# Batch 0 of a pooled-attention and feed-forward kernel: three fp32 loads on SyncE's queue, v in two loads, pooled products in bank tiles of their own

## The chip, the core and the metric

The kernel runs on one core of a Trainium2 chip. The metric is the device time of one execution in microseconds (us). The engines are named as in the profile: PE (TensorE, matrix products), DVE (VectorE), ACT (ScalarE), POOL (GpSimd) and SP (SyncE, which only issues transfers). Each engine works through its own list of instructions in order, and semaphores join the lists. Matrix products are written to PSUM[...]; DVE and ACT read them from there.

## The reference

Two steps follow one another. The first is attention with pooled keys and values. Eight batches of eight heads have 576 tokens of 64 numbers; eight neighbouring rows of k and of v are averaged, so that each head has 72 pooled rows.

```python
k_p = k.reshape(B, H, Sp, pool, D).mean(axis=3)
v_p = v.reshape(B, H, Sp, pool, D).mean(axis=3)
scores = scale * np.matmul(q, k_p.transpose(0, 1, 3, 2))
scores = scores - np.max(scores, axis=-1, keepdims=True)
attn = np.exp(scores)
attn = attn / (np.sum(attn, axis=-1, keepdims=True) + 1e-09)
return np.matmul(attn, v_p)
```

The second treats the 4608 tokens of 512 numbers as rows of x:

```python
h = x @ w_in            # 512 x 2048
g = h * np.cos(h)
return g @ w_out        # 2048 x 512
```

All inputs are fp32. The kernel computes with bf16 operands and fp32 sums.

## The kernel before, in words

The 4608 tokens are nine chunks of 512. For each chunk `t` the kernel does the up stage (`up_mm`, line 291, sixteen groups of four products of 128x128 by 512, two groups to a pair of banks `banks[fp % 3]`), the cosine on ACT and the product on DVE (`up_g`, line 301), and the down stage (`down_mm`, line 309, 64 products). The attention of batch `t + 1` is woven into the down stage of chunk `t` through the list `fill`, whose first entry is the number of the down product ahead of which a piece stands. The order of the work is written out by hand; no planner changes it.

**Batch 0 has nothing to hide behind.** Its attention is the head of the kernel (lines 396 to 420), and the change is there. The steps are these. `pool_k_mm` (line 150) multiplies k rows by a matrix of zeros and ones, `groups`, and so gives the pooled, transposed keys; one call treats two pairs of heads. The two heads of a pair lie in the lower and the upper 64 rows of the array. `put_kk` (line 128) copies the result from PSUM to `kk`, four copies to a call, since each head is wanted in both halves of the partitions. `q_transpose_mm` (line 189) transposes q in 18 blocks of 128 columns; blocks 0 to 8 are the first two head pairs. `scores` (line 204) multiplies and calls the exponential on ACT (line 218). `sums_first` (line 260) makes the sums of the exponentials and their inverse by a logarithm and an exponential on ACT (lines 270 and 271). `pool_v_mm` (line 160) pools v for all four head pairs at once into `vz`. `values_then` (line 274) multiplies by the pooled v, and DVE scales the result into `xT` (line 282). The four units of `us` are head pairs 0 and 1 for token segments 0 and 1, then head pairs 2 and 3 for both segments. `up_mm(0, 0, 0, 2)` and `up_mm(0, 1, 0, 2)` need only the first two units; the up products with `ki` 2 and 3 need the last two.

**Loads.** All loads but one go through POOL's queue (`nc.gpsimd.dma_start`), which turns fp32 into bf16 on the way. The one exception is the first half of k for batch 0: line 342 loads it as fp32 over SP's queue into the space of `g_sb`, which is not used until chunk 0's cosine, and ACT turns it into bf16 (line 343). POOL issues, in order: half of q, the constants for `groups` (lines 348 and 351), the second halves of k and of q, v, the identity, three parts of `w_in`, k and q of batch 1, the last part of `w_in`, the rest of q, `w_out` part 0, v of batch 1, two clearings of `kp2`, and `w_out` parts 1 to 3. Eight semaphores take turns on this queue, so each load waits, before it is issued, for the eighth load ahead of it. The loads are carried out in order by sixteen DMA engines.

`groups` is made on DVE (lines 361 to 365), ahead of the clearing of `vz[0]` and two small constants. `warm_up` (line 388) runs products on a constant tile whose result nobody reads.

Of the kernel before, what the change touches and what calls it, by code (L numbers as in the profile page):

```python
# [9 lines left out]
FP32 = mybir.dt.float32  # L10
# [4 lines left out]
POOL = 8  # L15
# [4 lines left out]
def kernel(  # L20
# [59 lines left out]
    def even_view(src, b, j0=0, j1=KCH):  # L80
        return src[b, 2 * j0:2 * j1].rearrange("(j a) (p t) d -> (a p) j (t d)", a=2, t=ROW)
# [43 lines left out]
    def v_part(b):  # L125
        return vz[b % 2][:, :, 0:4:3, :]

    def put_kk(b, ps, pj0, pj1, copy):
        dst = kk[b % 2].rearrange("p (j a) n -> p j a n", a=2)
        for a in range(2):  # L130
            for r in range(2):
                copy(out=dst[half[r], pj0:pj1, a, 0:Sp], in_=ps[half[a]])

    def pool_add(b, which):

        st = staged.pop((which, b))
# [10 lines left out]
            s = s.rearrange("p (j a) t d -> p j a t d", a=2)  # L147
            add(out=v_part(b), in0=s[..., 0, :], in1=s[..., 1, :], op=ADD)

    def pool_k_mm(b, bank, pj0, pj1):  # L150

        kb = staged["k", b]
        ps = bank[:, 0:(pj1 - pj0) * Sp].rearrange("p (j n) -> p j n", n=Sp)
        for pj in range(pj0, pj1):
            for t in range(ROW):
                for rows in half:
                    nc.tensor.matmul(ps[rows, pj - pj0, :], lhsT=kb[rows, pj, t, :], rhs=groups[rows, t, :],
                                     start=(t == 0), stop=(t == ROW - 1))
        return lambda copy: put_kk(b, ps, pj0, pj1, copy)

    def pool_v_mm(b, pair):
        vb = staged["v", b]
        for t in range(ROW):
            for hp, rows in enumerate(half):
                nc.tensor.matmul(pair[:Sp, hp, 0:KCH * D], lhsT=groups[rows, t, :], rhs=vb[rows, :, t, :],
                                 start=(t == 0), stop=(t == ROW - 1))
        nc.vector.tensor_copy(out=v_part(b).rearrange("p j a d -> p a j d"),
                              in_=pair[:Sp, :, 0:KCH * D].rearrange("p a (j d) -> p a j d", j=KCH))

    def k_transpose(b):  # L170
        nc.sync.dma_start_transpose(out=kk[b % 2], in_=kp2[b % 2].rearrange("p h s d -> p (h s d)"))
# [160 lines left out]


    EX = 5
    warm = consts.tile([128, 512], BF16, name="warm")
    nc.vector.memset(warm, 1.0)
    exp_tables()

    kv_even_tiles(0)
    q_tile(0)  # L340
    k_first = g_sb.rearrange("p f n -> p (f n)").bitcast(FP32)[:, 0:2 * ROW * D]
    nc.sync.dma_start(out=k_first.rearrange("p (j n) -> p j n", j=2), in_=even_view(k, 0, 0, 2))
    nc.scalar.copy(out=staged["k", 0][:, 0:2].rearrange("p j t d -> p (j t d)"), in_=k_first)
    load_even(staged["q", 0], 0, q, 0, 2)

    row_of = consts.tile([128, ROW], FP32, name="row_of")
    for rows in half:
# [4 lines left out]
                   allow_small_or_imprecise_dtypes=True)  # L352
    load_even(staged["k", 0], 0, k, 2, 4)
    load_even(staged["q", 0], 0, q, 2, 4)
    load_even(staged["v", 0], 0, v)
    identity = consts.tile([128, 128], BF16, name="identity")
    make_identity(nc, identity)
    dist = consts.tile([128, ROW, Sp], FP32, name="dist")
    sign = consts.tile([128, ROW, Sp], FP32, name="sign")
    groups = consts.tile([128, ROW, Sp], BF16, name="groups")  # L360
    nc.vector.tensor_tensor(out=dist, in0=row_of.unsqueeze(2).to_broadcast([128, ROW, Sp]),
                            in1=first_of.unsqueeze(1).to_broadcast([128, ROW, Sp]), op=mybir.AluOpType.subtract)
    nc.vector.scalar_tensor_tensor(out=sign, in0=dist, scalar=1.0 - POOL, in1=dist, op0=ADD,
                                   op1=mybir.AluOpType.mult)
    nc.vector.tensor_scalar(out=groups, in0=sign, scalar1=0.0, scalar2=None, op0=mybir.AluOpType.is_le)
    nc.vector.memset(vz[0], float(POOL))
    ones = consts.tile([128, D], BF16, name="ones")
    nc.vector.memset(ones, float(POOL))
    gate = consts.tile([1, 1], BF16, name="gate")
    half_pi = consts.tile([128, 1], FP32, name="half_pi")  # L370
    nc.vector.memset(half_pi, math.pi / 2.0)

    kv_even_tiles(1)
    q_tile(1)
# [5 lines left out]
    load_even(staged["q", 1], 1, q, 2, 4)  # L380
    load_w_out(0)
    load_even(staged["v", 1], 1, v)
    for i in range(2):
        nc.gpsimd.memset(kp2[i], 0.0)
    for cg in range(1, 4):
# [2 lines left out]
    def warm_up(n, bank):  # L388

        for i in range(n):  # L390
            nc.tensor.matmul(bank, lhsT=warm[:, 0:128], rhs=warm)

    vec, act = nc.vector.tensor_copy, nc.scalar.copy
    us = BY_HEADS

    warm_up(10, obanks[0])
    pool_k_mm(0, obanks[1], 0, 2)(vec)
    warm_up(2, banks[1][:, 0, :])
    puts = q_transpose_mm(0, banks[2][:, 0, :], 0, 5), q_transpose_mm(0, obanks[0], 5, 9)
    puts[0](vec)  # L400
    puts[1](act)
    warm_up(2, banks[1][:, 0, :])
    scores(0, us[0], banks[0])
    scores(0, us[1], banks[1])
    pool_k_mm(0, obanks[1], 2, 4)(vec)
    sums_first(0, us[0], banks[0][:, 0, :])
    puts = q_transpose_mm(0, banks[2][:, 0, :], 9, 14), q_transpose_mm(0, obanks[0], 14, 18)
    puts[0](vec)
    puts[1](act)
    sums_first(0, us[1], obanks[1])  # L410
    scores(0, us[2], banks[0])
    scores(0, us[3], banks[2])
    nc.vector.memset(vz[1], float(POOL))
    pool_v_mm(0, banks[1])
    sums_first(0, us[2], obanks[0])
    values_then(0, us[0], obanks[1])
    values_then(0, us[1], banks[1][:, 0, :])
    sums_first(0, us[3], banks[2][:, 0, :])
    values_then(0, us[2], obanks[1])
    values_then(0, us[3], obanks[0])  # L420
    up_mm(0, 0, 0, 2)
    up_mm(0, 1, 0, 2)
    sin_tables()
# [1 line left out]
    for t in range(NT):  # L425
        b = t + 1
        if t > 0:

            up_mm(t, 0, 0, 2)
            up_mm(t, 1, 0, 2)  # L430
        for fp in range(FFCH // 2):
            up_mm(t, fp, 2 if fp < 2 else 0)
            between = ()
            if t == 0:
                if fp == 4:
                    puts = pool_k_mm(1, obanks[0], 0, 2), pool_k_mm(1, obanks[1], 2, 4)
# [12 lines left out]
        mms = [(ms, fc) for ms in range(4) for fc in range(FFCH)]  # L449
        if t == 0:  # L450
            mms = [(ms, fc) for hm in range(2) for cg in range(4) for ms in range(2 * hm, 2 * hm + 2)
                   for fc in range(4 * cg, 4 * cg + 4)]


        def S_(n, bank):
            return lambda: scores(b, us[n], banks[bank])

        later = []

        def V_(n, bank, wait=None):  # L460
            return lambda: values(b, us[n], banks[bank], wait)

        fill = []
        if t < B:
            exp_tables()
            fill = [(1, lambda: scores(t, REST, banks[2])), (12, lambda: values(t, REST, banks[1]))]
        if t == 0:
            fill[1:] = [(2, S_(0, 0)), (8, lambda: pool_v_mm(1, banks[1])), (8, lambda: values(t, REST, banks[2])),
                        (11, S_(1, 0)), (13, V_(0, 1)), (18, S_(2, 2)), (21, V_(1, 0, later)), (26, S_(3, 1)),
                        (32, lambda: later.pop()()), (32, V_(2, 2)), (40, V_(3, 0))]  # L470
# [64 lines left out]
```

The softmax here doesn't subtract the row's maximum and nothing guards it: scores larger than these inputs give would overflow.

## Time and profile before

| What | Value |
|---|---|
| Median of five runs | 303.48 us (303.41 to 308.05) |
| The profiled execution | 303.48 us, of which its span 301.7 us |
| Granted TensorE clock | 1.0 over the span |
| PE busy | 291.4 us, 97% of the span |
| ACT, DVE, POOL busy | 205.9, 171.6, 129.9 us |
| First up product of chunk 0 | 17.42 us into the span |
| First down product of chunk 0 | 33.66 us into the span |
| HBM read, written | 36.70 MB, 9.44 MB |

The span counts from the first instruction of the profiled execution to its last. A timeline line gives the start and the duration, then engine, line, operation and tiles, the number of instructions merged into it, and in brackets for how long the engine was idle before it and what ended that. In a table of windows each engine has its busy time and number of instructions; the last two columns are the mean share of the sixteen DMA engines that had a packet under way and the bytes written per second. A casting load counts with its bf16 bytes, half of what it reads.

### The profile page before, as it was taken

What the parts mean: (1) busy time and instruction counts of PE and PEld (TensorE: products, weight loads), DVE (VectorE), ACT (ScalarE), POOL (GpSimd) and SP (SyncE); (2) the same over time, 40 slices, a digit from 0 to 9 for tenths busy, and PEclk for the clock granted to TensorE, in tenths of its full rate; (3) what the DMA queues carried; (4) which work ended last, traced back from release to release, by engine and by line L of the source; (5) the groups of instructions that cost most, each with busy time, mean ns of one, the idle gap of its engine ahead of it and who ended that gap; (6) DMA issues with size and microseconds to landing.
All of it is one profiled execution on the core that took longest, in us unless ns stands there. A gap on an engine that the chain in (4) does not pass through costs nothing.

```text
span 301.7 us, 4567 instructions
## 1 busy us (share of the span) xinstructions
PE 291.4 (97%) x1766; PEld 142.4 (47%) x1798; DVE 171.6 (57%) x211; ACT 205.9 (68%) x255; POOL 129.9 (43%) x92
## 2 busy tenths in 40 slices
PE   7799999999999999999999999999999999999994
PEld 2545544444544554455444544455445544444443
DVE  6558546574467446754675566654675476415612
ACT  3886897469866987688768877789578966506500
POOL 8553017984973398339823990399200000000000
PEclk9999999999999999999999999999999999999999
DMA  7999999739436951796069707791811130131032
GB/s 143 200 207 206 209 203 200 159 47 183 99 70 119 177 111 44 135 169 129 16 157 150 137 20 171 105 166 35 149 24 35 37 70 0 34 73 35 0 72 70
DMA packets 44005, 32.91 MB, mean 109 GB/s; under 512 B 22096, under 2 KB 39248, under 8 KB 43984
## 3 DMA queue, kind: packets, MB, share of 16 engines
q0 software_dynamic: 19744, 18.07, 38.2%
q1 hardware_dynamic: 24080, 14.42, 20.4%
q8 instruction: 14, 0.23, 0.3%
q10 hardware_dynamic: 160, 0.13, 0.2%
q14 instruction: 7, 0.06, 0.1%
HBM read 36.70 MB, written 9.44 MB: 153 GB/s over the span
## 4 chain that ended last, share of the span: by engine, by line
PE 83%; DMA 11%; POOL 2%; ACT 2%; issue 1%; DVE 0%; POOLq 0%; ACTq 0%
PE obank L310 38%; PE bank L297 37%; DMA w_out_sb<-in_moe_w_out_dram 6%; DMA w_in_sb<-in_moe_w_in_dram 5%; PE bank L241 5%; PE bank L211 3%; PE bank L328 1%; ACT ex L218 1%; POOL q_b L84 1%; POOL kv_st L84 1%; POOL w_in_sb L112 0%; ACT L285 0%; ACT cos L304 0%; POOL identity masks.py:197 0%; DVE o_sb L316 0%
## 5 line engine op out<-in xcount | busy, mean ns | idle before, releaser
L310 PE MATMUL obank<-w_out_sb,g_sb 128*128 128x512 bf16 x542 | 128.9, 379 | 1.0 <-DMA w_out_sb<-in_moe_w_out_dram 0.2
L297 PE MATMUL bank<-xT,w_in_sb 128*128 128x512 bf16 x563 | 125.9, 379 | 0.7
L304 ACT ACTIVATE cos<-bank,half_pi 128x1024 f32<-128x1024 f32 x72 | 79.2, 1112 | 59.8 <-PE bank L297 58.6
L307 DVE TENSOR_TENSOR g_sb<-bank,cos 128x1024 bf16<-128x1024 f32 x72 | 87.4, 1224 | 42.5 <-ACT cos L304 42.4
L297 PEld LDWEIGHTS <-w_in_sb 128*128 128x128 bf16 x576 | 56.1, 98 | 67.6 <-issue 1.6
L310 PEld LDWEIGHTS <-g_sb 128*128 128x128 bf16 x560 | 52.8, 98 | 57.0 <-issue 2.4
L252 DVE TENSOR_TENSOR xT<-bank,inv 64x512 bf16<-64x512 f32 (+1 forms) x72 | 45.3, 630 | 42.5 <-ACT inv L248 41.7
L141 POOL TENSOR_TENSOR kv_st<-kv_st 72x2048 f32<-72x2048 bf16 x12 | 48.8, 4063 | 34.7 <-DMA kv_st<-in_k_dram 34.7
L247 ACT ACTIVATE lnc<-bank 64x512 f32<-64x512 f32 (+1 forms) x72 | 39.2, 544 | 3.0 <-PE bank L241 1.7
L218 ACT ACTIVATE ex<-bank 72x1024 bf16<-72x1024 f32 (+1 forms) x40 | 35.0, 928 | 8.5 <-PE bank L211 8.4
L316 DVE COPY o_sb<-obank 128x512 f32<-128x512 f32 x35 | 23.6, 690 | 30.1 <-PE obank L310 29.7
L142 POOL TENSOR_TENSOR kv_st<-kv_st 72x1024 f32<-72x1024 f32 x12 | 28.2, 2350 | 1.0
L248 ACT ACTIVATE inv<-lnc 128x512 f32<-128x512 f32 (+1 forms) x36 | 21.0, 582 | 1.2
L241 PE MATMUL bank<-ex,vz 72*128 72x256 bf16 (+1 forms) x176 | 20.0, 243 | 0.5 <-ACT ex L218 0.4
L241 PEld LDWEIGHTS <-vz 72*128 72x128 bf16 x176 | 13.6, 97 | 9.9 <-issue 0.6
L145 POOL TENSOR_TENSOR kp<-kv_st 72x512 bf16<-72x512 f32 x12 | 14.9, 1266 | 0.5
L211 PE MATMUL bank<-qT,kk 64*72 64x256 bf16 (+1 forms) x192 | 13.4, 252 | 0.9 <-ACT qT L193 0.5
L211 PEld LDWEIGHTS <-kk 64*72 64x72 bf16 x192 | 7.5, 109 | 10.6 <-issue 8.4
L285 ACT ACT_TABLE_LOAD x9 | 11.5, 1283 | 0.9 <-PEq L519 0.8
L499 POOL COPY gate<-kk 1x1 bf16<-1x1 bf16 x5 | 0.9, 182 | 25.6 <-DMA kk<-kp 25.6
L288 ACT ACT_TABLE_LOAD x9 | 11.5, 1283 | 0.2
L84 POOL DMA_DIRECT2D q_b<-in_q_dram x10 | 7.7, 770 | 3.0 <-DMA w_in_sb<-in_moe_w_in_dram 1.4
(55 smaller groups left out, 88.8 us busy)
## 6 DMA issues: line engine op xcount, KB each, us to landing
out_dram<-o_sb SPq DMA_DIRECT2D x70, 128.0 KB, 2.4
kv_st<-in_v_dram POOLq DMA_DIRECT2D x8, 576.0 KB, 13.4
kv_st<-in_k_dram POOLq DMA_DIRECT2D x7, 576.0 KB, 7.7
q_b<-in_q_dram POOLq DMA_DIRECT2D x6, 576.0 KB, 9.6
w_in_sb<-in_moe_w_in_dram POOLq DMA_DIRECT2D x4, 512.0 KB, 13.4
w_out_sb<-in_moe_w_out_dram POOLq DMA_DIRECT2D x4, 512.0 KB, 18.6
q_b<-in_q_dram POOLq DMA_DIRECT2D x4, 288.0 KB, 12.1
g_sb<-in_k_dram SPq DMA_DIRECT2D x1, 576.0 KB, 3.5
```

Of the source, the lines that this page charges most:

```text
L141: add(out=s, in0=x[:, :, 0:4, :], in1=x[:, :, 4:8, :], op=ADD)
L142: add(out=s[:, :, 0:2, :], in0=s[:, :, 0:2, :], in1=s[:, :, 2:4, :], op=ADD)
L211: nc.tensor.matmul(pair[:Sp, bank, c:c + n].rearrange("p (g n) -> p g n", n=64), lhsT=kk[b % 2][half[r], h0 + i, 0:Sp], rhs=att["qT", b][h ...
L218: nc.scalar.activation(out=ex[:, 0:nh * n].rearrange("p (a n) -> p a n", a=2), in_=pair[:Sp, :, 0:nh * n // 2], func=ACTF.Exp, scale=scale ...
L241: nc.tensor.matmul(pair[:, hp, (i // 2) * n:(i // 2 + 1) * n], lhsT=vz[b % 2][:, pj, 2 * hp:2 * hp + 2, :].rearrange("p a d -> p (a d)"), ...
L247: nc.scalar.activation(out=lnc[half[1 - hp]], in_=pair[half[1 - hp], hp, 0:w], func=ACTF.Ln)
L252: nc.vector.tensor_mul(out=x_out(b, u, half[hp]), in0=cols(pair[half[hp], hp, :], u), in1=cols(inv[half[1 - hp]], u))
L297: nc.tensor.matmul(h[:, j, :], lhsT=w_in_sb[fc // 4][:, ki, (fc % 4) * 128:(fc % 4 + 1) * 128], rhs=xT[:, ki, t * TILE:(t + 1) * TILE], st ...
L304: nc.scalar.activation(out=cos, in_=h, func=ACTF.Sin, bias=half_pi[:, :1])
L307: nc.vector.tensor_mul(out=g_sb[:, 2 * fp:2 * fp + 2, :], in0=h, in1=cos)
L310: nc.tensor.matmul(o, lhsT=g_sb[:, fc, ms * 128:(ms + 1) * 128], rhs=w_out_sb[fc // 4][:, fc % 4, :], start=(fc == 0), stop=(fc == FFCH - 1))
L316: nc.vector.tensor_copy(out=o[:, 0:n], in_=ps)
```

## The change

The first half of q for batch 0 moves from POOL's queue to SP's. It arrives as fp32 in the same borrowed space, and DVE turns it into bf16 in two instructions, one for each head pair, that stand after the first pooled product in DVE's order. The first half of k becomes two loads on SP's queue and two conversions on ACT, one for each head pair. v of batch 0 becomes two loads on POOL's queue, two calls of `pool_v_mm`, and two copies for each call.

`pool_k_mm` and `pool_v_mm` take a list of bank tiles, one for each head of a pair. Before, both heads of a k product went to one bank in different partitions. The copies are then one function for each head, which DVE and ACT can share. The copies of the second half of q's transposes are both on DVE; before, one was on ACT. For batch 1 one call of `pool_k_mm` treats all four pairs, with four copies of 288 columns in place of eight of 144.

The order of the head changes: the second pooled k product comes after the first sums, v's first half is pooled ahead of the last two scores, and the values of the first two units come ahead of the sums of the last two. Bank tiles are handed out anew. Of the fourteen warm-up products, eight in place of ten are at the start and two more stand ahead of the first sums. On DVE the clearing of `vz[0]` and two constants move ahead of `groups`. The clearing of `vz[1]` moves from DVE to POOL, between v of batch 1 and the clearing of `kp2`.

```diff
-    def pool_k_mm(b, bank, pj0, pj1):
+    def pool_k_mm(b, ps, pj0, pj1):
...
-        ps = bank[:, 0:(pj1 - pj0) * Sp].rearrange("p (j n) -> p j n", n=Sp)
+        ps = [p[half[a], 0:(pj1 - pj0) * Sp].rearrange("p (j n) -> p j n", n=Sp) for a, p in enumerate(ps)]
...
+        def put(a):
+            def go(copy):
+                for r in range(2):
+                    copy(out=dst[half[r], pj0:pj1, a, 0:Sp], in_=ps[a])
+            return go
+
+        return put(0), put(1)
...
+    def pool_v_mm(b, ps, pj0=0, pj1=KCH):
...
+                nc.tensor.matmul(ps[hp], lhsT=groups[rows, t, :], rhs=vb[rows, pj0:pj1, t, :],
                                  start=(t == 0), stop=(t == ROW - 1))
...
+        for hp in range(2):
+            nc.vector.tensor_copy(out=v_part(b)[:, pj0:pj1, hp, :], in_=ps[hp].rearrange("p (j d) -> p j d", d=D))
...
-    nc.sync.dma_start(out=k_first.rearrange("p (j n) -> p j n", j=2), in_=even_view(k, 0, 0, 2))
-    nc.scalar.copy(out=staged["k", 0][:, 0:2].rearrange("p j t d -> p (j t d)"), in_=k_first)
-    load_even(staged["q", 0], 0, q, 0, 2)
...
+    for j in range(2):
+        nc.sync.dma_start(out=raw[:, j:j + 1], in_=even_view(k, 0, j, j + 1))
+    nc.sync.dma_start(out=raw[:, 2:4], in_=even_view(q, 0, 0, 2))
+
+    def cast_first(which, copy, j):
+        copy(out=staged[which, 0][:, j].rearrange("p t d -> p (t d)"), in_=raw[:, 2 * (which == "q") + j])
+
+    for j in range(2):
+        cast_first("k", nc.scalar.copy, j)
...
-    load_even(staged["v", 0], 0, v)
+    load_even(staged["v", 0], 0, v, 0, 2)
+    load_even(staged["v", 0], 0, v, 2, 4)
...
+    nc.gpsimd.memset(vz[1], float(POOL))
...
-    warm_up(10, obanks[0])
-    pool_k_mm(0, obanks[1], 0, 2)(vec)
-    warm_up(2, banks[1][:, 0, :])
-    puts = q_transpose_mm(0, banks[2][:, 0, :], 0, 5), q_transpose_mm(0, obanks[0], 5, 9)
+    warm_up(8, obanks[0])
+    puts = pool_k_mm(0, obanks, 0, 2)
+    for j in range(2):
+        cast_first("q", vec, j)
+    puts[0](act)
+    puts[1](vec)
+    warm_up(2, banks[2][:, 0, :])
+    puts = q_transpose_mm(0, banks[1][:, 0, :], 0, 5), q_transpose_mm(0, banks[0][:, 0, :], 5, 9)
     puts[0](vec)
     puts[1](act)
...
+    scores(0, us[0], banks[2])
+    scores(0, us[1], banks[0])
+    warm_up(2, obanks[1])
+    sums_first(0, us[0], obanks[0])
+    for put in pool_k_mm(0, [banks[1][:, i, :] for i in range(2)], 2, 4):
+        put(vec)
     sums_first(0, us[1], obanks[1])
...
+    for put in [q_transpose_mm(0, banks[0][:, i, :], 9 + 5 * i, 14 + 4 * i) for i in range(2)]:
+        put(vec)
+    pool_v_mm(0, obanks, 0, 2)
+    scores(0, us[2], banks[2])
+    scores(0, us[3], banks[1])
+    values_then(0, us[0], obanks[0])
+    values_then(0, us[1], obanks[1])
+    pool_v_mm(0, (banks[0][:, 0, :], banks[0][:, 1, :]), 2, 4)
+    sums_first(0, us[2], banks[2][:, 0, :])
+    sums_first(0, us[3], banks[1][:, 0, :])
+    values_then(0, us[2], obanks[0])
+    values_then(0, us[3], obanks[1])
...
-                    puts = pool_k_mm(1, obanks[0], 0, 2), pool_k_mm(1, obanks[1], 2, 4)
+                    puts = pool_k_mm(1, obanks, 0, 4)
```

More of the change, by code (lines that the diff above doesn't have):

```diff
@@ L126, in v_part @@
         return vz[b % 2][:, :, 0:4:3, :]
[L128 to L132, printed above, removed]
     def pool_add(b, which):
@@ L148, in pool_add @@
             add(out=v_part(b), in0=s[..., 0, :], in1=s[..., 1, :], op=ADD)
-    def pool_k_mm(b, bank, pj0, pj1):
+    def pool_k_mm(b, ps, pj0, pj1):
         kb = staged["k", b]
-        ps = bank[:, 0:(pj1 - pj0) * Sp].rearrange("p (j n) -> p j n", n=Sp)
+        ps = [p[half[a], 0:(pj1 - pj0) * Sp].rearrange("p (j n) -> p j n", n=Sp) for a, p in enumerate(ps)]
         for pj in range(pj0, pj1):
             for t in range(ROW):
-                for rows in half:
-                    nc.tensor.matmul(ps[rows, pj - pj0, :], lhsT=kb[rows, pj, t, :], rhs=groups[rows, t, :],
+                for a in range(2):
+                    nc.tensor.matmul(ps[a][:, pj - pj0, :], lhsT=kb[half[a], pj, t, :], rhs=groups[half[a], t, :],
                                      start=(t == 0), stop=(t == ROW - 1))
-        return lambda copy: put_kk(b, ps, pj0, pj1, copy)
-    def pool_v_mm(b, pair):
+        dst = kk[b % 2].rearrange("p (j a) n -> p j a n", a=2)
+        def put(a):
[5 more added lines that the diff above has]
+    def pool_v_mm(b, ps, pj0=0, pj1=KCH):
         vb = staged["v", b]
+        ps = [p[:Sp, 0:(pj1 - pj0) * D] for p in ps]
         for t in range(ROW):
             for hp, rows in enumerate(half):
-                nc.tensor.matmul(pair[:Sp, hp, 0:KCH * D], lhsT=groups[rows, t, :], rhs=vb[rows, :, t, :],
+                nc.tensor.matmul(ps[hp], lhsT=groups[rows, t, :], rhs=vb[rows, pj0:pj1, t, :],
                                  start=(t == 0), stop=(t == ROW - 1))
-        nc.vector.tensor_copy(out=v_part(b).rearrange("p j a d -> p a j d"),
-                              in_=pair[:Sp, :, 0:KCH * D].rearrange("p a (j d) -> p a j d", j=KCH))
+        for hp in range(2):
+            nc.vector.tensor_copy(out=v_part(b)[:, pj0:pj1, hp, :], in_=ps[hp].rearrange("p (j d) -> p j d", d=D))
     def k_transpose(b):
@@ L334 @@
     EX = 5
-    warm = consts.tile([128, 512], BF16, name="warm")
+    warm = consts.tile([128, 128], BF16, name="warm")
     nc.vector.memset(warm, 1.0)
@@ L340 @@
     q_tile(0)
-    k_first = g_sb.rearrange("p f n -> p (f n)").bitcast(FP32)[:, 0:2 * ROW * D]
-    nc.sync.dma_start(out=k_first.rearrange("p (j n) -> p j n", j=2), in_=even_view(k, 0, 0, 2))
-    nc.scalar.copy(out=staged["k", 0][:, 0:2].rearrange("p j t d -> p (j t d)"), in_=k_first)
-    load_even(staged["q", 0], 0, q, 0, 2)
+    raw = g_sb.rearrange("p f n -> p (f n)").bitcast(FP32)[:, 0:KCH * ROW * D].rearrange("p (i n) -> p i n", i=KCH)
+    for j in range(2):
[5 more added lines that the diff above has]
+        cast_first("k", nc.scalar.copy, j)
     row_of = consts.tile([128, ROW], FP32, name="row_of")
@@ L360 @@
     groups = consts.tile([128, ROW, Sp], BF16, name="groups")
[L361 to L365, printed above, removed]
     nc.vector.memset(vz[0], float(POOL))
@@ L371 @@
     nc.vector.memset(half_pi, math.pi / 2.0)
+    nc.vector.tensor_tensor(out=dist, in0=row_of.unsqueeze(2).to_broadcast([128, ROW, Sp]),
+                            in1=first_of.unsqueeze(1).to_broadcast([128, ROW, Sp]), op=mybir.AluOpType.subtract)
+    nc.vector.scalar_tensor_tensor(out=sign, in0=dist, scalar=1.0 - POOL, in1=dist, op0=ADD,
+                                   op1=mybir.AluOpType.mult)
+    nc.vector.tensor_scalar(out=groups, in0=sign, scalar1=0.0, scalar2=None, op0=mybir.AluOpType.is_le)
     kv_even_tiles(1)
@@ L390, in warm_up @@
         for i in range(n):
-            nc.tensor.matmul(bank, lhsT=warm[:, 0:128], rhs=warm)
+            nc.tensor.matmul(bank.rearrange("p (a n) -> p a n", a=4), lhsT=warm,
+                             rhs=warm.unsqueeze(1).to_broadcast([128, 4, 128]))
     vec, act = nc.vector.tensor_copy, nc.scalar.copy
     us = BY_HEADS
-    warm_up(10, obanks[0])
-    pool_k_mm(0, obanks[1], 0, 2)(vec)
-    warm_up(2, banks[1][:, 0, :])
-    puts = q_transpose_mm(0, banks[2][:, 0, :], 0, 5), q_transpose_mm(0, obanks[0], 5, 9)
+    warm_up(8, obanks[0])
@@ L400 @@
+    puts = pool_k_mm(0, obanks, 0, 2)
[5 more added lines that the diff above has]
+    puts = q_transpose_mm(0, banks[1][:, 0, :], 0, 5), q_transpose_mm(0, banks[0][:, 0, :], 5, 9)
     puts[0](vec)
     puts[1](act)
[L402 to L407, printed above, removed]
@@ L408 @@
-    puts[0](vec)
-    puts[1](act)
-    sums_first(0, us[1], obanks[1])
[L411 to L420, printed above, removed]
+    warm_up(2, banks[2][:, 0, :])
+    scores(0, us[0], banks[2])
@@ L467 @@
         if t == 0:
-            fill[1:] = [(2, S_(0, 0)), (8, lambda: pool_v_mm(1, banks[1])), (8, lambda: values(t, REST, banks[2])),
+            fill[1:] = [(2, S_(0, 0)), (8, lambda: pool_v_mm(1, [banks[1][:, i, :] for i in range(2)])), (8, lambda: values(t, REST, banks[2])),
                         (11, S_(1, 0)), (13, V_(0, 1)), (18, S_(2, 2)), (21, V_(1, 0, later)), (26, S_(3, 1)),
```

## The prediction

> **What bounds the kernel now.** I read the page's engine totals first, then its chain, then the chain again in order of time, then the timeline of the head, then windows over the DMA engines. The page and its chain:
>
> ```profile
> PE 291.4 (97%) x1766; PEld 142.4 (47%) x1798; DVE 171.6 (57%) x211; ACT 205.9 (68%) x255; POOL 129.9 (43%) x92
> ...
> PE 83%; DMA 11%; POOL 2%; ACT 2%; issue 1%; DVE 0%; POOLq 0%; ACTq 0%
> ```
>
> PE is the bound from the first up product on. The change touches the head, so what matters is how early PE is let go, and the DMA 11%. In order of time, the chain around 40 us:
>
> ```profile
> 21.85 18.86 DMA w_out_sb<-in_moe_w_out_dram
> 40.72 0.04 issue
> 40.76 0.59 PE obank L310 x2
> ```
>
> Up to 40.7 us the chain is not PE but the row of loads: part 2 of w_out lands at 40.71 and PE waits. In the trace that product would have followed its neighbour by 0.215, at 40.42, and began at 40.755: 0.34 lost. The product that reads part 1 began at 37.806 where the row of products would have put it at 37.64: 0.17 lost. So PE has 0.17 + 0.34 = **0.51 us of slack** against the loads. Part 3 landed at 43.26 and cost nothing. If the head lets PE go x later and the loads land d earlier, the end moves by the larger of x − 0.51 and −d. The head in the timeline:
>
> ```profile
> 4.31 1.15 ACT L343 CAST kv_st<-g_sb 128x1152 bf16<-128x1152 f32 x1 [2.27 <-DMA g_sb<-in_k_dram]
> 4.61 0.74 DVE L365 TENSOR_SCALAR groups<-sign 128x648 bf16<-128x648 f32 x1
> ...
> 6.68 1.28 DVE L132 CAST kk<-obank 64x144 bf16<-64x144 f32 x4 [0.18 <-PE obank L157]
> ...
> 7.64 0.45 PE L192 MATMUL bank<-identity,q_b 128*128 128x128 bf16 x5 [0.47 <-DMA q_b<-in_q_dram]
> ...
> 8.13 0.49 DVE L193 COPY qT<-bank 128x640 bf16<-128x640 bf16 x1 [0.17 <-PE bank L192]
> ...
> 9.40 1.93 ACT L218 ACTIVATE ex<-bank 72x1024 bf16<-72x1024 f32 x2 [0.46 <-PE bank L211]
> ...
> 14.02 1.91 ACT L218 ACTIVATE ex<-bank 72x1024 bf16<-72x1024 f32 x2
> ...
> 18.40 0.69 DVE L282 TENSOR_TENSOR xT<-obank,inv 128x512 bf16<-128x512 f32 x1 [0.37 <-ACT inv L271]
> ```
>
> The first exponential waits for q, which landed at 7.59 (issued at 1.26, 6.3 to landing). From 9.40 ACT is nearly full to 18.37; the last scaling ends at 19.09 and the first up product that needs it starts at 19.14. That point is **9.74 us after the first exponential**, and it is what the head hands to PE. The DMA engines:
>
> ```profile
> 2.50:3.50 1.00, 1.00 (x4) 0.30 (x2) 0.62 (x1) 0.00 (x0) 0.93 (x3) 1.00 1.03 387
> 4.00:8.00 4.00, 3.53 (x50) 1.60 (x49) 3.53 (x9) 1.15 (x1) 3.92 (x7) 1.00 1.05 135
> 8.00:9.40 1.40, 1.33 (x15) 0.69 (x13) 0.49 (x1) 0.58 (x1) 1.40 (x3) 1.00 1.15 184
> 9.40:17.40 8.00, 6.16 (x106) 4.23 (x104) 4.64 (x10) 7.87 (x12) 2.99 (x5) 1.00 1.23 207
> ```
>
> All busy in every row, but POOL's casting loads ran at 135 and 184 GB/s early and at 207 later. Against 207 that is 4.0 x 72 + 1.4 x 23 = 320 KB, **1.55 us lost**. SP's plain load ran at 387.
>
> **The change part by part.**
>
> *k in two loads, groups later on DVE.* The conversion of 1152 columns (1.15) becomes two of 576; from 1.15 and the 0.59 of a 512-column ACT row I take 0.65 each. groups now comes after clearings of 0.91 + 0.11 + 0.06, but its iotas no longer stand behind q's 0.87 issue on POOL, so it ends near 4.6 in place of 5.35. Pooling can begin near 4.7, before at 5.84. This is worth nothing by itself: its cover is q's arrival, which comes later. If q came before 5 us, that 1.1 would count.
>
> *q over SP.* SP's three issues at 0.46 (its row: 0.46) end near 2.1. The k load of 590 KB landed at 4.25; at 387 GB/s another 590 KB takes 1.5, so q lands no earlier than 5.8. The second half of k, now first on POOL's queue, has as much to read. Here a rule speaks against the change: the Trainium skill, "DMA: Bandwidth & Descriptors", section "Queues, rings and completion order", has each DMA engine take turns between the queues that have work for it, packet by packet. No stretch of this trace has two long loads on two queues. By the row alone q lands at 5.8; by the rule, with even turns, both loads finish together, 1180 KB at 387 GB/s after 4.25 or so, at 7.3 at most. If the slow early rate belongs to the engines and not to POOL's queue, 1180 KB at twice 135 GB/s takes 4.4, and q lands at 8.6. I take **6.3**: turns, but with POOL's queue leaving some of its own unused as it did between 4 and 8 us.
>
> *Two conversions on DVE.* No row shows a DVE copy from SBUF fp32 to bf16. The nearest is groups, 648 columns, same types and memory, 0.744; for 576 that is 0.67. The skill, "VectorE: DVE Perf Modes", section "The perf-mode tier table", gives such copies two elements per cycle, and gives it to operations like groups as well, which the 0.744 contradicts (648 columns at one per cycle of 0.96 GHz are 0.675). By the rule it would be (288 + 66)/0.96 = 0.37. I take 0.67, since the row is the nearer; the rule is worth 0.6 for the pair.
>
> *To the first exponential.* After q lands: 0.05, then 0.62 + 0.67 for the conversions, then the two copies of pooled k that now stand behind them on DVE (2 x 0.32), the transposed q (0.49), and 0.48 for score products and the step to ACT (8.94 to 9.40 before). Sum 2.95; before, from 7.59 to 9.40, it was 1.81. **The first exponential is at 9.25 by the row (8.65 by the rule), before 9.40.**
>
> *From there to the last scaling.* Exponential 1.02, step 0.05, sums' four products 0.21: the second pooled k starts at +1.28 and ends at +2.06 (0.78, its row). Four copies at 0.32 and the two q copies, both on DVE (0.49 + 0.43), end at +4.25; scores and step give the third exponential at +4.72 (before +4.62). Taking 0.57 off ACT buys nothing, because ACT then waits for DVE. Behind those six copies on DVE stand v's first copies, and for these wait the values of units 0 and 1, and behind them on PE the pooling of v's rest and the sums. ACT's remaining row took 18.37 − 14.02 = 4.35; I add 0.1 for the sums that now queue behind the values. Inverse ready at +9.17, scaling 0.69 and two steps: +9.97, before +9.74. So x = 9.25 + 9.97 − 19.14 = **+0.08**. In general x is q's landing minus 6.22 by the row, minus 6.82 by the rule.
>
> *Covers.* v's first half is wanted near 12.9 (when the second logarithm frees its bank), the whole landed at 13.50 before, so half of it lands in time even at the old pace. Each v copy of 256 columns costs about 0.42 against half of 0.687; hidden unless DVE is late by more than 0.5. Clearing vz[1] takes 0.91 off DVE where it was idle, and adds about 0.97 (POOL's clearing row) ahead of w_out part 1, issued at 19.33 and landing at 37.76; seven loads stand in the queue then, so nothing moves. The issue count of POOL stays the same: q's half leaves, v's second comes. In batch 1 four copies of 288 columns replace eight of 144: about 0.3 less on DVE and ACT, beside up products.
>
> *The loads.* Bytes read stay the same. d is at most 1.55 plus 0.2 (SP's packets took 93 ns against 107 for the same source bytes), at least about −0.3 if mixing costs something. Half of the loss: **d = 0.8**. Then the end moves by the larger of 0.08 − 0.51 = −0.43 and −0.8: −0.43. The profiled execution is 303.48 (301.70 of span and 1.78 around it), equal to the median. It gives 303.05; I write **303.0**.
>
> **Rivals.** *Early q and quick conversions* (30%): q at 6.2 and 0.37 each, x = −0.62, the limit is −1.13 from PE and −0.8 from the loads: 302.7, down to 302.1 where d is 1.4. For it: POOL's queue is the slow one between 4 and 8 us. Against: the groups row. *q late* (slower, 20%): the slow stretch belongs to the engines, or turns go against SP. q at 7.8 gives x = +1.58 and +1.07: 304.6. It decides from q at 6.73 by the row, and passes 0.2% from 7.35. For it: DMA busy over 1.0 in all rows while moving half. Against: 387 GB/s just before. *Loads don't move* (12%): d = 0, x below 0.5: 303.5. *Clock* (6%, slower): the first ten warm-up products were spaced 0.43 and later ones 0.215. With eight of them the pooling may fall into the slow time, and PE's longer wait for q may let the clock fall back; some 60 head products at double spacing add about 1 us: 304.5.
>
> **How the numbers follow.** The main case has 32%. 0.2% is 0.6 us, about what a measurement tells from no change. Faster: the first rival (30%) and 5% of the main case, 0.35. Same: the rest of the main case and the unmoved loads, 0.38. Slower: q late, the clock and what is left, 0.27. The range goes from 302.1 (1.4 gained) to 304.7 (q near 7.9).
>
> **What would show it.** q's landing between 5.8 and 7.3, conversions of 0.67 or 0.37, the first exponential near 9.2, the third 4.7 later, the product with ki 2 near 19.2, and waits for w_out near 38 and 40 us that are smaller. I am wrong if q lands past 7.3, if the third exponential comes over 5.5 after the first, or if w_out part 2 lands later than 40.7.

## The result, and the profile after

| | before | after |
|---|---|---|
| Median | 303.43 us (47 runs) | 306.39 us (27 runs) |
| Ratio of the undisturbed runs, 95% interval | | 1.0062 (1.0041 to 1.0083) |
| The profiled execution, its span | 303.48, 301.7 us | 307.1, 305.3 us |
| PE's last product ends at | 297.75 us | 301.53 us |

The change makes the kernel slower. The forecast was 303.0 with a range of 302.1 to 304.7, so it was wrong. The changed kernel's own runs stand at two levels, four of 27 at 302.3 to 303.3 and the others, like the profiled execution, at 305.4 to 308.9 (five of the 47 runs before took 306.4 to 308.3); the ratio leaves the longest runs out and so lies below the ratio of the medians.

The page of the changed kernel: engine totals, the granted clock and DMA share in forty slices, and the shares of the chain.

```profile
PE 293.0 (96%) x1785; PEld 143.3 (47%) x1816; DVE 170.5 (56%) x213; ACT 206.1 (68%) x255; POOL 130.5 (43%) x93
...
PEclk9799999999999999999999999999999999999999
DMA  6999999359507970979177916691611120031022
...
PE 90%; ACT 4%; DMA 3%; issue 1%; DVE 1%; SPq 0%; ACTq 0%
```

The DMA share of the chain fell from 11% to 3%. The end no longer waits for the row of w_out loads. It waits for PE, and PE waits for a short piece of DMA at the head. The second digit of the clock is a 7, so PE ran slower there. The chain in order of time (start, duration, what):

```profile
1.68 8.55 DMA g_sb<-in_q_dram
10.23 0.02 issue
10.25 0.47 DVE q_b L353
10.72 0.05 issue
10.77 1.14 PE bank L197 x9
...
13.38 1.93 ACT ex L223 x2
...
22.69 0.70 DVE xT L287
23.39 0.04 issue
23.44 0.59 PE bank L302 x2
```

q's first half, issued on SP's queue at 1.68, landed at **10.23**. Before, on POOL's queue, it had landed at 7.59. All that follows is the row of steps that the prediction gave, but from a start 3.9 us later than it had assumed. The timeline of the same stretch:

```profile
3.65 1.36 ACT L353 CAST kv_st<-g_sb 128x576 bf16<-128x576 f32 x2 [1.62 <-DMA g_sb<-in_k_dram]
...
4.59 1.29 PE L152 MATMUL obank<-groups,kv_st 64*64 64x72 bf16 x36
...
10.25 0.83 DVE L353 CAST q_b<-g_sb 128x576 bf16<-128x576 f32 x2 [5.94 <-DMA g_sb<-in_q_dram]
...
10.77 1.14 PE L197 MATMUL bank<-identity,q_b 128*128 128x128 bf16 x9 [3.92 <-DVE q_b L353]
...
18.20 1.93 ACT L223 ACTIVATE ex<-bank 72x1024 bf16<-72x1024 f32 x2 [0.46 <-PE bank L216]
...
23.44 7.10 PE L302 MATMUL bank<-xT,w_in_sb 128*128 128x512 bf16 x32 [0.37 <-DVE xT L287]
...
41.93 0.81 PE L315 MATMUL obank<-w_out_sb,g_sb 128*128 128x512 bf16 x3
```

k's first pair was converted from 3.65 on (4.31 before) and k was pooled from 4.59 on (5.84 before). (The changed kernel also fills a warm-up tile of 128 columns in place of 512, which is not among the changes named above; its warm-up began at 1.07, before at 1.47.) Then DVE stood idle for 5.94 us and PE for 3.92, both for q. The first product that needs the last scaling began at 23.44, before at 19.14: x = **+4.30**. The down product at 41.93, the first to read part 1 of w_out, shows no wait any more. With 0.51 us of slack used up, the end should move by 4.30 − 0.51 = 3.79. PE's last product ended 301.53 − 297.75 = 3.78 later.

The DMA windows of the changed kernel (window, then busy time by engine; the last two columns are the share of DMA engines with a packet under way and GB/s written):

```profile
4.00:5.50 1.50, 1.50 (x32) 0.91 (x32) 0.31 (x1) 1.00 (x2) 1.43 (x4) 1.00 0.89 201
5.50:7.50 2.00, 1.35 (x16) 0.37 (x10) 0.00 (x0) 0.54 (x2) 2.00 (x4) 1.00 0.93 172
7.50:9.40 1.90, 0.00 (x0) 0.00 (x0) 0.00 (x0) 0.00 (x0) 0.50 (x1) 1.00 1.13 215
```

Between 4 and 5.5, 201 GB/s were written, where SP's plain load had moved at 387 before, and the share of busy engines was below one. POOL's first data packet began at 5.18, so up to then SP's loads had the engines to themselves.

### The profile page after: what moved, and what is told of

It is laid out like the page before. It is cut to its first block, busy times and chain, and to the rows that moved or that the text cites. A ratio compares the mean times of both kernels' runs of the same rounds, so it can differ in the third digit from the quotient of the medians.

```text
span 305.3 us, 4614 instructions
## 1 busy us (share of the span) xinstructions
PE 293.0 (96%) x1785; PEld 143.3 (47%) x1816; DVE 170.5 (56%) x213; ACT 206.1 (68%) x255; POOL 130.5 (43%) x93
## 4 chain that ended last, share of the span: by engine, by line
PE 90%; ACT 4%; DMA 3%; issue 1%; DVE 1%; SPq 0%; ACTq 0%
PE bank L302 40%; PE obank L315 38%; PE bank L246 5%; PE bank L216 3%; DMA g_sb<-in_q_dram 3%; ACT ex L223 2%; PE bank L333 1%; ACT lnc L275 1%; ACT inv L276 1%; PE obank L152 0%; ACT L290 0%; PE bank L197 0%; ACT cos L309 0%; PE bank L170 0%; PE obank L197 0%
## 5 line engine op out<-in xcount | busy, mean ns | idle before, releaser
L103 POOL DMA_DIRECT2D kv_st<-in_v_dram x6 | 5.1, 844 | 11.6 <-PE bank L170 11.6
```

## The experiments

The theory that the first four runs led to: q is late because it is the **third** load on SP's queue (which also has it issued later, at 1.68 in place of 1.28). It is unfinished when the casting loads of POOL's queue reach the engines at about 5.2, and from then on it shares with them. Rivals: the new order of products is at fault; SP's queue loses to POOL's wherever q stands; q's packets are slow by themselves; PE's clock is at fault. The table holds what was read from each trace; "SP loads" counts the loads on SP's queue, and "third" says what is third.

| Kernel | SP loads | q landed | first exponential | last product ended | median |
|---|---|---|---|---|---|
| before | 1 | 7.59 (POOL) | 9.40 | 297.75 | 303.43 |
| after | 3, third q | 10.23 | 13.38 | 301.53 | 306.39 |
| after, second trace | 3, third q | 10.11 | 13.26 | 301.67 | 307.22 |
| after, q back on POOL's queue | 2 (k, k) | 7.03 (POOL) | 8.84 | 297.25 | 303.57 |
| only q moved to SP | 2 (k, q) | 5.92 | 9.26 | 297.09 | 302.56 |
| the same, a second time | 2 (k, q) | 5.95 | 9.26 | 297.06 | 302.47 |
| after, k in one load | 2 (k, q) | 5.94 | 10.02 | 298.16 | 303.13 |
| only q moved, k in two loads | 3, third q | 9.17 | 12.46 | 300.30 | 305.87 |
| after, q ahead of k's second pair | 3, third k | 4.99 | 12.68 | 300.80 | 306.85 |
| after, POOL held | 3, third q | 6.88 | 10.98 | 299.12 | 304.87 |
| after, POOL held, identity first | 3, third q | 6.89 | 10.13 | 299.30 | 304.54 |
| after, sixteen more warm-ups | 3, third q | 8.87 | 11.41 | 299.56 | 305.22 |
| only q moved, q's conversions on DVE and ACT | 2 (k, q) | 5.79 | 9.48 | 297.32 | 303.30 |
| the same, k's conversions shared too | 2 (k, q) | 6.04 | 8.76 | 296.95 | 302.81 |

The runs of before beside them had medians of 303.31 to 303.38.

**The change without its move of q.** q's first half goes back to POOL's queue, ahead of the constants.

```diff
-    nc.sync.dma_start(out=raw[:, 2:4], in_=even_view(q, 0, 0, 2))
+    load_even(staged["q", 0], 0, q, 0, 2)
...
-    for j in range(2):
-        cast_first("q", vec, j)
```

> Only q's first half goes back to POOL's queue, ahead of the constants, where it stood before; k in two loads, v in two, the bank tiles and the new order stay. Theory A (the cost is q's landing at 10.23 on SP's queue, because engines that have not finished q when POOL's loads start hardly serve SP any more): q lands near 7.6 as before, the first exponential follows within 2 us at 9.2 to 9.6, the ki 2 product 10 us later near 19.4, PE's gap stays under 2.5 us and the clock at 1.0; time 302.9 to 303.8. Rival R (the new order of the head or the bank tiles cost it): q early, but the time stays above 305.

303.57 us, ratio 0.9993 (0.9971 to 1.0016); the traced execution took 302.72. The third exponential came 4.82 after the first and the product with ki 2 came 10.05 after it, just as in the changed kernel. So the new order, the bank tiles and v in two loads cost about 0.3 against the 9.74 of before. An earlier start paid for it here, and on the whole they come out even. The order is not the cause of the loss.

**The move of q alone.** The kernel before, with q's first half on SP's queue behind the one load of k, and the two conversions on DVE.

```diff
-    load_even(staged["q", 0], 0, q, 0, 2)
+    nc.sync.dma_start(out=q_first, in_=even_view(q, 0, 0, 2))
...
+    for j in range(2):
+        vec(out=staged["q", 0][:, j].rearrange("p t d -> p (t d)"), in_=q_first[:, j])
```

> The kernel before with one part alone: q's first half over SP's queue behind the one k load, turned into bf16 by two DVE copies that stand ahead of the copies of pooled k. Theory A: q lands late here too, at 8.5 to 10.5, the first exponential 2.6 to 3.2 later at 11.5 to 13.4, and the time is 305.5 to 307.5. Rival R (the order and the bank tiles cost it): near the kernel before, 303 to 304.

302.56 us, ratio 0.9951 (0.9918 to 0.9985): faster than both kernels. Its timeline:

```profile
5.95 1.10 DVE L401 CAST q_b<-g_sb 128x576 bf16<-128x576 f32 x2 [1.10 <-DMA g_sb<-in_q_dram]
...
9.26 1.02 ACT L218 ACTIVATE ex<-bank 72x1024 bf16<-72x1024 f32 x1 [0.94 <-PE bank L211]
...
18.25 0.69 DVE L282 TENSOR_TENSOR xT<-obank,inv 128x512 bf16<-128x512 f32 x1 [0.51 <-ACT inv L271]
```

q landed at 5.92, on the same queue on which the changed kernel got it at 10.23. I had expected 8.5 to 10.5: the rival that SP's queue loses to POOL's wherever q stands falls. Its DMA window 4.0 to 5.5 reads

```profile
4.00:5.50 1.50, 1.50 (x5) 0.44 (x3) 0.85 (x3) 0.94 (x1) 1.43 (x4) 1.00 1.07 355
```

355 GB/s, where the changed kernel wrote 201. The row of loads gained too: part 2 of w_out landed at 39.83, before at 40.71, and no down product waits. Most of the gain is there. q came 1.67 earlier, but its conversions and the copies of k stand between it and the scores, so that the last scaling began only 0.15 earlier (18.25, before 18.40). By the prediction's rule the end moves by −0.15 − 0.51 = −0.66, and PE's last product ended 0.66 earlier. A repeat without an edit:

> The kernel with only q's first half moved to SP's queue once more, without an edit. If its gain is real, the time is 302.3 to 302.9 with a ratio below 0.998; if the 302.56 was chance, it is 303 to 303.5, the same as before.

302.47 us (22 runs, 302.15 to 302.75), ratio 0.9966 (0.995 to 0.9982). The gain is real, 0.8 us between the medians.

**One line, both ways.** In the changed kernel k's two loads become one; in the kernel with q alone moved, k's one load becomes two. Nothing else differs.

```diff
-    for j in range(2):
-        nc.sync.dma_start(out=raw[:, j:j + 1], in_=even_view(k, 0, j, j + 1))
+    nc.sync.dma_start(out=raw[:, 0:2], in_=even_view(k, 0, 0, 2))
```

> The changed kernel with k's first half in one load over SP in place of two, so that q's first half is SP's second load and is issued at about 1.28 in place of 1.68; the order of the products, the bank tiles, v in two loads and q's conversions on DVE stay. Theory (q loses because its packets are still in the engines when POOL's loads start at about 5): q lands near 6.0 in place of 10.2, the first exponential comes 3.1 later at 9.1, the product with ki 2 near 19.2, and the time is 302.5 to 303.3, some 3 below the changed kernel. Rival (q over SP loses to POOL's loads whatever its place): q lands past 8.5 again, and the time stays at 305 to 306.5.

> The kernel with only q's first half moved to SP's queue (302.56), and now also k's first half in two loads, so that q is SP's third load; nothing else differs. Theory (the third place on SP's queue is what makes q late): q lands between 8.5 and 10.3 in place of 5.92, the first exponential is at 11.8 to 13.6, and the time is 304.5 to 306.5. Rival (the late q belongs to the new order of the products or to v in two loads): q lands near 6, and the time stays within 0.4 of 302.6.

The first: 303.13 us, ratio 0.9989 (0.9979 to 1.0); the traced execution took 303.62, and ten of its 20 runs 302.2 to 302.9. The second: 305.87 us, ratio 1.0096 (1.0075 to 1.0117). In the changed kernel with k in one load:

```profile
5.30 1.32 PE L152 MATMUL obank<-groups,kv_st 64*64 64x72 bf16 x36 [0.64 <-ACT kv_st L352]
5.96 1.02 DVE L352 CAST q_b<-g_sb 128x576 bf16<-128x576 f32 x2 [1.64 <-DMA g_sb<-in_q_dram]
```

and in the kernel with q alone moved and k in two loads:

```profile
9.19 0.83 DVE L403 CAST q_b<-g_sb 128x576 bf16<-128x576 f32 x2 [4.33 <-DMA g_sb<-in_q_dram]
```

The same bytes in two loads or in three: q lands near 6 or past 9, and the time goes by 3.3 us with it, whatever the order of products. This is the cause, shown in both directions; whether it is the third place or the issue 0.4 us later was not tried apart. The first exponential of the first kernel missed its expectation (10.02, not 9.1), because PE was slow: 36 pooling products took 1.32 us and nine transposes 1.17, against 0.77 and 0.68 in the changed kernel with q back on POOL's queue.

**Which load is third.** SP's order is turned to k, q, k.

```diff
+    nc.sync.dma_start(out=raw[:, 0:1], in_=even_view(k, 0, 0, 1))
     nc.sync.dma_start(out=raw[:, 2:4], in_=even_view(q, 0, 0, 2))
+    nc.sync.dma_start(out=raw[:, 1:2], in_=even_view(k, 0, 1, 2))
```

> The changed kernel with the order of SP's three loads turned: k's first head pair, then q's first half, then k's second head pair. Theory (whichever load is third is caught by POOL's packets, whatever it holds): q lands near 5.5 to 6.3, but k's second pair, half as large, lands at 7 to 9.2 in place of 4.32; the second half of the first k pooling then waits for it, the first exponential comes about 3 after that, at 10 to 12, and the time is 303.5 to 305. Rival (q's own packets are slow wherever they stand): q lands past 8.5, k's second pair after it, and the time is 305.5 or more.

306.85 us, ratio 1.0096 (1.0071 to 1.0121). q landed at 4.99, and now k's second pair, half as large, waited in its place:

```profile
5.01 1.02 DVE L353 CAST q_b<-g_sb 128x576 bf16<-128x576 f32 x2 [0.71 <-DMA g_sb<-in_q_dram]
...
8.05 0.67 ACT L353 CAST kv_st<-g_sb 128x576 bf16<-128x576 f32 x1 [3.76 <-DMA g_sb<-in_k_dram]
8.78 0.55 PE L152 MATMUL obank<-groups,kv_st 64*64 64x72 bf16 x18 [3.44 <-ACT kv_st L353]
```

q's packets are not slow by themselves; the last load on SP's queue is caught. The time missed its expectation by some 2 us: I had put the first exponential at 3 after k's landing, and it took 4.65, since the conversion, the pooling, the copies of k and the slow transposes (1.17) all stand behind it.

**POOL's loads held back.** In the changed kernel a one-element copy on POOL waits for k's second load before POOL issues its own loads; in a second version POOL makes the identity ahead of that.

```diff
+    hold = consts.tile([1, 1], FP32, name="hold")
+    nc.gpsimd.tensor_copy(out=hold, in_=raw[0:1, 1, 0:1])
     load_even(staged["k", 0], 0, k, 2, 4)
```

> POOL's first load waits, through a one-element copy on POOL, until SP's second k load has landed (4.3 in the changed kernel), so SP has the engines alone for q. Theory A: q lands by 6.5 at the latest, the first exponential comes at 8.4 to 9.0, and PE is let go near 18.5 to 19; the price is that POOL's row of loads starts about 2 us after 4.4, so w_out part 2 lands near 41.5 to 42.5 and sets the end: 304.0 to 305.2. Rival B (the slow stretch belongs to the engines or to q's first packets, whatever else is queued): q lands at 8 or later, first exponential past 10.5, time 306 or more.

> The changed kernel with POOL making the identity first and then waiting for k's second load before it issues its own loads, so that SP's three loads have the engines to themselves until about 6. Theory (q waits because POOL's packets are served ahead of what is left of it): q lands near 6.8 in place of 10.2, its transposes no longer wait for the identity, the first exponential is near 10, and the product with ki 2 near 20; the loads come 1 later than in the changed kernel at the head, so the time is 303.3 to 304.5. Rival (q's lateness is in its own long packets): q lands past 8.5 and the time stays above 305.

304.87 us, ratio 1.0059 (1.0045 to 1.0073), and 304.54 us, ratio 1.0029 (1.0009 to 1.0049). q landed at 6.88 and 6.89 with the same three loads (expected: by 6.5, and near 6.8). In the first, q's transposes waited for something else:

```profile
6.91 0.93 DVE L353 CAST q_b<-g_sb 128x576 bf16<-128x576 f32 x2 [2.60 <-DMA g_sb<-in_q_dram]
...
8.39 1.12 PE L197 MATMUL bank<-identity,q_b 128*128 128x128 bf16 x9 [2.30 <-POOL identity masks.py:199]
```

The identity stood behind the held loads on POOL. The second version removes that wait, and then the loads set the end, as they had been moved back by the hold:

```profile
39.72 0.81 PE L315 MATMUL obank<-w_out_sb,g_sb 128*128 128x512 bf16 x3 [0.89 <-DMA w_out_sb<-in_moe_w_out_dram]
```

So q's lateness has two parts. A third load costs 0.9 us without POOL's loads beside it (about 5.95 to 6.89): with the identity first, thirteen of the sixteen engines had finished their part of q by 5.86, as with two loads, and the other three finished at 6.74, 6.78 and 6.89. POOL's loads add 2.0 to 3.3 (8.87 to 10.23 in the four traces with three loads, q third and POOL not held).

**PE kept busy.** Sixteen more warm-up products ahead of q's transposes in the changed kernel.

```diff
-    warm_up(2, banks[2][:, 0, :])
+    warm_up(18, banks[2][:, 0, :])
     puts = q_transpose_mm(0, banks[1][:, 0, :], 0, 5), q_transpose_mm(0, banks[0][:, 0, :], 5, 9)
```

> Sixteen more warm-up products ahead of q's transposes, 3.4 us at full clock, so that PE does not idle while q is missing. Theory A: q lands near 10 as in the changed kernel, the clock stays up, and the step from q's landing to the first exponential falls from 3.15 to about 2.4 and the rest of the head by 0.1 to 0.3: 305.3 to 305.9, so the clock is about a quarter of the loss. Rival C (the fallen clock is the main loss): 303.5 or less. If q lands before 8.5 in a run, the extra products themselves cost up to 2 us there.

305.22 us, ratio 1.0069 (1.0045 to 1.0093), four runs.

```profile
8.90 0.83 DVE L353 CAST q_b<-g_sb 128x576 bf16<-128x576 f32 x2 [4.59 <-DMA g_sb<-in_q_dram]
9.65 0.67 PE L197 MATMUL bank<-identity,q_b 128*128 128x128 bf16 x9
...
11.41 1.93 ACT L223 ACTIVATE ex<-bank 72x1024 bf16<-72x1024 f32 x2 [0.47 <-PE bank L216]
```

The transposes took 0.67 in place of 1.14, and the first exponential followed q's landing by 2.54 in place of 3.15. Keeping PE busy is thus worth 0.6 us of the loss. The rest of this run's advantage is q, which happened to land at 8.87.

**The changed kernel once more**, without an edit:

> The changed kernel once more, without an edit, beside the three others on the same chip, for a second trace. If q's landing near 10.2 is the rule, the first exponential is again at 13 to 13.5 and the time 305 to 306.5. If it varies with the execution, q lands anywhere between 6 and 10.3 and the first exponential follows it by 3.1; where it lands near 6, the time is about 302.5.

307.22 us, ratio 1.0124 (1.0106 to 1.0143), four runs. q landed at 10.11 and the first exponential came 3.15 later, so the first trace was no accident. What q does in the rare executions of 302.3 us stays open, as no trace of one was had; that it then lands near 6 is only argued.

**Going on from q alone.** First q's second conversion moves to ACT; then k's second conversion moves to DVE as well, with eight warm-ups in place of ten.

```diff
-        vec(out=staged["q", 0][:, j].rearrange("p t d -> p (t d)"), in_=q_first[:, j])
+        (vec, act)[j](out=staged["q", 0][:, j].rearrange("p t d -> p (t d)"), in_=q_first[:, j])
```

> The kernel with only q's first half moved to SP's queue (302.56), with the second of q's two conversions on ACT beside the first on DVE. If PE's start is still what sets the end, the first exponential comes 0.5 earlier, near 8.75, and the time falls by 0.2 to 0.5, to about 302.2. If the row of loads sets it by now (part 1 of w_out landed at 37.25 there and PE had no wait for it), the head gains 0.5 and PE waits for w_out again: 302.5, no change.

> The kernel with only q's first half moved to SP's queue, with the conversions shared: k's first head pair on ACT and its second on DVE, q's first on DVE and its second on ACT, and eight warm-up products in place of ten, so that the pooling of k can start at about 5.2 in place of 5.84. If the head still sets PE's start, the first exponential comes near 8.7 (9.26 with q alone on SP's queue); w_out's loads then leave about 0.24 of it, and the time is 302.2 to 302.5. If the clock of PE falls in the longer gap, or the loads set the end, it is 302.6 to 303.2, no better than q alone on SP's queue.

303.30 us, ratio 0.9978 (0.9952 to 1.0004), and 302.81 us, ratio 0.9983 (0.997 to 0.9995). The first missed its expectation of 302.2 to 302.5. In its trace the pooling of k took 1.29 (0.81 with q alone moved), and the copies of k waited for it, so PE's last product ended at 297.32 in place of 297.09. PE's work up to that pooling is the same in both kernels, so the edit does not explain it. The second did bring the first exponential to 8.76 and the first up product from 17.14 to 16.64. But then the loads took it back:

```profile
37.37 0.81 PE L310 MATMUL obank<-w_out_sb,g_sb 128*128 128x512 bf16 x3 [0.22 <-DMA w_out_sb<-in_moe_w_out_dram]
```

Of 0.50 us, 0.1 was left: PE's last product ended at 296.95 in place of 297.06. In that execution, the longest of its 20 (302.48 to 303.32), the last store on ACT's queue landed 3.1 us after its issue in place of 2.2, which is why its time is nonetheless longer. In the first it was 2.8. Whether the edits have a part in that is open. By its median, q alone on SP's queue stays the quickest of all the kernels.

## Why the prediction was wrong

**The step that failed** is the first of its list: k in two loads, "This is worth nothing by itself." It was costed as a matter of conversions and of when pooling can begin. What it does to the queue was left out: it makes q the third load in place of the second. With k in one load q landed at 5.92 to 5.95, the prediction's lower bound of 5.8 and better than its 6.3; with k in two, and POOL not held, at 8.87 to 10.23.

**q's landing, 6.3, measured 10.23.** Two things made the difference. The packet records show both; SP's packets of 2304 bytes normally take 0.093 us.

| Trace | SP packets not begun when POOL's eleventh began | its time | time of SP's packets over 0.093 each, sum of 16 engines |
|---|---|---|---|
| only q moved | 6 of 512 | 5.38 | 5.2 us |
| after, k in one load | 14 | 5.29 | 5.6 us |
| only q moved, k in two | 80 | 5.26 | 12.5 us |
| after | 117 | 5.39 | 14.4 us |
| after, second trace | 73 | 5.27 | 12.1 us |

First, each load begins with packets of 0.15 to 1.6 us on many engines. With two loads these fall at 1.9 to 2.7 and at 3.1 to 3.7 us. A third load has a third such group, at about 4 to 6. Three loads cost some 7 to 9 us more than two over sixteen engines, and 2 to 5 more with POOL held (7.4 and 10.0). The packets begun from 3.9 to 5.3 took 2.5 to 6.1 us too long with three loads, 2.2 and 4.0 with POOL held, and at most 0.1 with two, so this group belongs to the third load and not to POOL's packets; why it is so long is open. It is very unevenly spread: in the changed kernel, by the sixteen updates of q's semaphore, eight engines had finished their part of q by 5.98, and the others finished at 7.16, 7.92, 8.61, 8.65, 8.90, 8.92, 10.11 and 10.23. Second, the engines that still held q when POOL's packets came shared with them. Here the rule weighed in the prediction (the Trainium skill, "DMA: Bandwidth & Descriptors", section "Queues, rings and completion order") holds. From 9.0 to 9.8, when two engines still held q, eight of SP's packets were begun, one per 0.2 us on each engine; 0.106 for SP's and 0.107 for POOL's is 0.213. What was wrong was to work with sixteen alike engines. By that I got 7.3 at most, and 8.6 from the slow early rate; but a load lands when its last engine is done. At that pace sixteen packets take 16 x 0.213 = 3.4 us, so an engine that had hardly begun its part of q at 6.4 ends near 9.8, where the last packet did end (the records don't name the engine, so this is worked out and not read).

**Conversions, 0.67 each, measured 0.46** in the changed kernel (two in 0.83). There the rule of two elements per cycle (0.37) was nearer than the row that I took; with q alone moved (two in 1.10) the row was. The row itself changed: groups took 0.74 before and 0.50 here, so it had not measured the operation alone. The gain of 0.4 was used up by PE.

**To the first exponential, 2.95, measured 3.15.** The rival on PE's clock took place inside this step. After 3.92 us idle, nine transposes took 1.14 in place of 0.67 and two warm-ups 1.06 in place of 0.60, and the granted clock was 0.79 from 9.4 to 17.4. The Trainium skill, "TensorE: Matmul & The Clock Gate", Part 1, has PE fall to half its clock after an idle window of about 3.4 us, and says that the number of slow products varies from run to run. The 3.92 agrees, but a shorter wait was enough elsewhere. With POOL held and the identity first, PE was idle for 1.28, and the granted clock was 0.50 (in the second line, a row of windows, the third number from the end):

```profile
7.43 1.23 PE L197 MATMUL bank<-identity,q_b 128*128 128x128 bf16 x9 [1.28 <-DVE q_b L353]
...
7.50:10.80 3.30, 3.30 (x20) 1.62 (x21) 1.50 (x4) 1.26 (x2) 3.30 (x6) 0.50 1.14 169
```

PE's pace at the very head changed from trace to trace: k's pooling took 1.29 in the changed kernel with no gap ahead of it, 1.32 with k in one load after a gap of 0.64, and 0.77 with q back on POOL's queue after a gap of 0.68. The granted clock reads 1.00 there in all three, so it does not show the cause, which stays open.

**From there to the product with ki 2, 9.97, measured 10.06**, and the third exponential 4.72, measured 4.82. This step was right, in the changed kernel and in the one with q back on POOL's queue.

**The loads, d = +0.8, measured −0.75, −0.37 and −0.34** for parts 1 to 3 of w_out (38.51, 41.08 and 43.60). With q alone moved they landed 0.51, 0.88 and 0.94 earlier, near the forecast. In the changed kernel k's second half on POOL's queue was late as well, and POOL waited for it 2.70 us before issuing its ninth load, so that all that follows was issued later. It cost nothing, as PE was later still.

**The rule for the end**, the larger of x − 0.51 and −d, was right: 3.79 against 3.78. The rival "q late" is what happened, from the point it gave (q at 6.73), with its size off: 7.8 was assumed. The range ended at q near 7.9. It should have reached further, since the prediction had itself noted that no stretch of the trace showed two long loads on two queues.

## What to carry to other kernels

Count the loads ahead of a critical load on its queue, not just their bytes: splitting an earlier load to start its consumer sooner can cost the load behind it far more, and one that is unfinished when another queue's long loads arrive lands with its slowest engine. Make a single part of a large change alone before giving up on it; here the move of q by itself is worth 0.8 us, and the split of k beside it costs 3.3. After speeding up the head, look at once at what then waits, as half a microsecond came down to 0.1 at the next load.

## What the runs showed of the hardware that was not expected

- Each further load on SP's queue begins with long packets (up to 1.6 us in place of 0.093). Over sixteen engines their excess sums to 3.7 us with the one load of the kernel before, 5.2 to 6.2 with k and q in two, 12.1 to 14.4 with three, and 7.4 and 10.0 with three and POOL held.
- POOL's casting loads started the later, the more SP's queue held. In the kernel before, the first casting packet came 1.6 us after the end of its load's issue (2.13 to 3.69). With q on SP's queue too it came 2.3 to 2.9 us after (from 2.30 to 4.57 at the earliest and 5.20 at the latest), and with POOL held until k had landed 0.7 us after (5.45 to 6.15).
- Two DVE conversions of 576 fp32 columns to bf16 took 0.83 us in the changed kernel and 1.10 with q alone moved; the same instruction that makes groups took 0.74 before and 0.50 after. The pair took 0.93 to 1.10 in the six traces in which POOL was issuing loads when it began, and 0.83 in the four in which it was not; but groups took 0.50 beside such an issue, so the cause is not shown.
- After PE's last product, which an output copy and store follow, the span went on for 3.7 to 3.9 us in twelve traces, but for 4.3 and 4.6 in the two kernels with shared conversions.
